# The output projection of a decode step turned over: wo as the stationary operand, its own PSUM columns, and no wait for the row maximum

## Chip, cores, metric

One NeuronCore of a Trainium2 chip. The metric is the device time of one execution in microseconds (us); the median of several is quoted.

## The reference

Two batches, one query token each, 32 heads of 128, a cache of 4096 keys. The gate mixes attention with a small feed-forward.

```python
q = (x @ wq).reshape(B, 1, 32, 128)                 # D = 512
scores = einsum("bhqd,bhkd->bhqk", q, k_cache) * 128**-0.5
o = einsum("bhqk,bhkd->bhqd", softmax(scores), v_cache)
a = o.reshape(B, 1, 4096) @ wo                      # the output projection, 4096 x 512
b = relu(x @ w1) @ w2                               # Dff = 1376
g = sigmoid((x * gate_w).sum(-1, keepdims=True))
out = g * a + (1 - g) * b
```

K and V are 1 MiB per batch and head, 134 MB together; all loads are 146 MB.

## The kernel before

There are 64 items (batch, head). Even items ("G") take their scores on GpSimd (product with a broadcast q) and VectorE (sum), odd items ("P") on TensorE (transposes of K, evictions, matmuls). (An eviction copies a matmul's result out of PSUM; a slot is a buffer that one item's K or V is loaded into.) The engines run one tick per item; item `i` is transposed at tick `i`, its V product comes at tick `i + 4`, and its head is projected at tick `i + 5` if `i` is of the second batch. So all 32 projections fall on ticks 37 to 68. SyncE issues K into 8 slots, ScalarE issues V into 4.

```python
def pe_AO(pe, h):                       # output projection of one head, both batches
    ...                                 # waits for both scaled outputs and for wo
    wait(pe, semGmax, mrow_emitted[0])  # the row maximum must have left psR
    if ao_emitted[0] >= 1:
        wait(pe, semAOacc, ao_emitted[0])
    pe.matmul(psR[32:32 + Bn, 0:Dout], Osb[:, h, :], wo_sb[:, h, :],
              start=True, stop=True).then_inc(semAO, 1)

def pe_MROW(pe, qi):                    # row of partial maxima, into the same psR
    wait(pe, semRmax, qi + 1); wait(pe, semGmax, qi)
    if ao_emitted[0] >= 1:
        wait(pe, semAOacc, ao_emitted[0])
    ...

def dve_AOacc(dve):                     # a_sb[2, 512] += psR
    ...
# TensorE, tick t: T(t) blocks 0,1 | scores(t-1) | T block 2 | MROW(t-2) | MBC(t-3)
#                  | T block 3 | PV(t-4) | AO
# VectorE, tick t: eviction, reductions of item t-1, row max, GMAX(t-2),
#                  OSC(t-4) (reciprocal, scaling), AOacc
# feed-forward, second layer, once at tick 1:
for fc in range(FC):                    # 11 matmuls, 512 moving columns
    pe.matmul(psS[1][0:Bn, 0:Dout], Hsb[0:m, fc, :], w2_sb[0:m, fc, :], ...)

def issue_V(eng, i):                    # on ScalarE's queue, at tick i + 1
    wait(eng, semPV, (i - NVS + 1) * rep)      # slot freed by its V product; NVS = 4
    eng.dma_start(Vs[i % NVS], ...)
def issue_K(eng, i):                    # on SyncE's queue
    knat_slot_free_wait(eng, i)         # slot freed by item i - 8; NKS = 8
    eng.dma_start(Knat[i % NKS], ...)
```

Of the kernel before, what the change touches and what calls it, by code (L numbers as in the profile page):

```python
# [6 lines left out]
ACT = mybir.ActivationFunctionType  # L7
ALU = mybir.AluOpType
AX = mybir.AxisListType
BF16 = mybir.dt.bfloat16  # L10
# [19 lines left out]
def _build(nc, A_x, A_k_cache, A_v_cache, A_wq, A_wo, B_w1, B_w2, gate_w, out,  # L30
# [9 lines left out]
    assert Hq * Dh == HqDh and Hkv * rep == Hq  # L40
    assert Dout <= 512 and D <= 512 and Bn <= 32
    NDC = D // 128
# [4 lines left out]
    NI = Bn * Hkv  # L47
# [7 lines left out]
    NMC = 16  # L55
    MBC0, OT0, DEN0 = 128, 128 + NMC, 128 + 2 * NMC
    inv = 1.0 / math.sqrt(Dh)

# [29 lines left out]
    with es:  # L88
# [28 lines left out]
        x_sb = sb([Bn, D], BF16, "x_sb")  # L117
        gw_sb = sb([Bn, D], BF16, "gw_sb")
        zt = sb([Bn, 4], FP32, "zt")
        bffn = sb([Bn, Dout], FP32, "bffn")  # L120
        a_sb = sb([Bn, Dout], FP32, "a_sb")
        tmp_f = sb([Bn, Dout], FP32, "tmp_f")
        junk = sb([Bn, max(D, Dout)], BF16, "junk")
        outsb = junk[:, 0:Dout]

# [43 lines left out]
        semAOacc = sem("semAOacc")  # L169
        semFin = sem("semFin")  # L170

        block = es.enter_context(nc.Block())
# [20 lines left out]
        def wait(eng, s, v):  # L193
            if v > 0:
                eng.wait_ge(s, v)
# [113 lines left out]
        @block.sync  # L309
        def _(sync):  # L310
            sync.dma_start(x_sb[0:Bn, :], A_x[:, 0, :]).then_inc(semX, 16)
            gw2 = gate_w.rearrange("(o d) -> o d", o=1)
            for b in range(Bn):
                sync.dma_start(gw_sb[b:b + 1, :], gw2[0:1, :]).then_inc(semX, 16)
            for dc in range(0, NDC, 2):
                sync.dma_start(wq_sb[dc][:, :], A_wq[dc * 128:(dc + 1) * 128, :]).then_inc(semWq[dc], 16)
            sync.dma_start(w1_sb[:, :, :], B_w1.rearrange("(c p) f -> p c f", p=128)).then_inc(semW1, 16)
            for t in range(T0, T1):
                issue_tick(sync, "S", t)
            wait(sync, semFin, 2)  # L320
            sync.dma_start(out[:, 0, :], outsb[0:Bn, :]).then_inc(semOut, 16)
            wait(sync, semOut, 16)
# [54 lines left out]

        def pe_AO(pe, h):
            for i in ao_items(h):
                for qi in qis_of_item(i):  # L380
                    wait(pe, semO, qi + 1)
            wait(pe, semWo[h // HO], 16)
            wait(pe, semGmax, mrow_emitted[0])
            if ao_emitted[0] >= 1:
                wait(pe, semAOacc, ao_emitted[0])
            pe.matmul(psR[32:32 + Bn, 0:Dout], Osb[:, h, :], wo_sb[:, h, :],  # L386
                      start=True, stop=True).then_inc(semAO, 1)
            ao_emitted[0] += 1
# [3 lines left out]
        def pe_MROW(pe, qi):  # L392
            wait(pe, semRmax, qi + 1)
            wait(pe, semGmax, qi)
            if ao_emitted[0] >= 1:
                wait(pe, semAOacc, ao_emitted[0])
            if qi == 0:
                wait(pe, semF1b, 2)
            pe.matmul(psR[0:1, 0:128], rmaxb[:, qi:qi + 1], ident_b[:, :],  # L399
                      start=True, stop=True).then_inc(semMrow, 1)  # L400
            mrow_emitted[0] += 1
# [10 lines left out]
        def pe_PV(pe, qi):  # L412
            i = qi // rep
            s = i % NVS
            par = qi % 2
            k = col_k(qi)
            es_ = qi % NES
            wait(pe, semExp, qi + 1)
            wait(pe, semV[s], 16 * (i // NVS + 1))
            for jj in range(J):  # L420
                pe.matmul(psO[par][:, OT0 + k:OT0 + k + 1], Vs[s][:, jj, :],  # L421
                          E[:, es_, jj:jj + 1], start=(jj == 0), stop=(jj == J - 1))
            pe.matmul(psO[par][:, DEN0 + k:DEN0 + k + 1], ones_b[:, :],  # L423
                      rowsum[:, qi:qi + 1], start=True, stop=True).then_inc(semPV, 1)
# [58 lines left out]

        def dve_AOacc(dve):
            k = aoacc_emitted[0]
            wait(dve, semAO, k + 1)
            if k == 0:
                dve.tensor_copy(out=a_sb[0:Bn, :], in_=psR[32:32 + Bn, 0:Dout]).then_inc(semAOacc, 1)
            else:
                wait(dve, semAOacc, k)  # L490
                dve.tensor_tensor(out=a_sb[0:Bn, :], in0=a_sb[0:Bn, :], in1=psR[32:32 + Bn, 0:Dout],  # L491
                                  op=ALU.add).then_inc(semAOacc, 1)
            aoacc_emitted[0] += 1
# [59 lines left out]
        def _(pe):  # L553
            wait(pe, semX, 16 * (1 + Bn))
            wait(pe, semSetup, 3)
            last = None
            for c in range(NDC):
                last = pe.matmul(psR[:, Bn * c:Bn * c + Bn], x_sb[0:Bn, c * 128:(c + 1) * 128],
                                 ident_b[0:Bn, 0:Bn], start=True, stop=True)
            last.then_inc(semXT, 1)  # L560
            wait(pe, semXT, 2)
            for dc in range(NDC):
                wait(pe, semWq[dc], 16)
            for h in range(Hq):
                for dc in range(NDC):
                    last = pe.matmul(psQB[:, Bn * h:Bn * h + Bn],
                                     wq_sb[dc][:, h * 128:(h + 1) * 128],
                                     xT_sb[:, dc, :], start=(dc == 0), stop=(dc == NDC - 1))
            last.then_inc(semQP, 1)

            def pe_FFN(pe):
                wait(pe, semW1, 16)
                wait(pe, semXT, 2)
                ll = None
                for fc in range(FC):
# [8 lines left out]
                if FC > 1:  # L584
                    wait(pe, semW2b, 16)
                for fc in range(FC):
                    m = 128 if fc < FC - 1 else last_m
                    ll = pe.matmul(psS[1][0:Bn, 0:Dout], Hsb[0:m, fc, :], w2_sb[0:m, fc, :],  # L588
                                   start=(fc == 0), stop=(fc == FC - 1))
                ll.then_inc(semF2, 1)  # L590

            for t in range(T0, T1):
# [17 lines left out]
                for h in ao_tick.get(t, []):  # L610
                    pe_AO(pe, h)
                if t == FFN_TICK:
                    pe_FFN(pe)
            for t in sorted(ao_tick):
                if t >= T1:
                    for h in ao_tick[t]:
                        pe_AO(pe, h)

        @block.vector
        def _(dve):  # L620
# [3 lines left out]
                            ).then_inc(semXT, 1)  # L624
            wait(dve, semX, 16 * (1 + Bn))
            dve.tensor_tensor_reduce(out=junk[0:Bn, 0:D], in0=x_sb[0:Bn, :], in1=gw_sb[0:Bn, :],
                                     scale=1.0, scalar=0.0, op0=ALU.mult, op1=ALU.add,
                                     accum_out=zt[0:Bn, 0:1]).then_inc(semG, 1)
            wait(dve, semQP, 1)
# [4 lines left out]
            def dve_FFN(dve):  # L634
# [7 lines left out]
                wait(dve, semF2, 1)  # L642
                dve.tensor_copy(out=bffn[0:Bn, :], in_=psS[1][0:Bn, 0:Dout]).then_inc(semF2b, 1)

            for t in range(T0, T1):
# [14 lines left out]
                for qi in qis_of_item(t - 2):  # L660
                    dve_GMAX(dve, qi)
                for qi in qis_of_item(t - 4):
                    dve_OSC(dve, qi)
                for h in ao_tick.get(t, []):
                    dve_AOacc(dve)
                if t == FFN_TICK:
                    dve_FFN(dve)
            for t in sorted(ao_tick):
                if t >= T1:
                    for h in ao_tick[t]:  # L670
                        dve_AOacc(dve)
            wait(dve, semG, 2)
            dve.tensor_scalar_add(out=zt[0:Bn, 2:3], in0=zt[0:Bn, 1:2], scalar1=1.0).then_inc(semG, 1)
            wait(dve, semG, 3)
            dve.reciprocal(out=zt[0:Bn, 3:4], in_=zt[0:Bn, 2:3]).then_inc(semG, 1)
            wait(dve, semAOacc, Hq)
            wait(dve, semF2b, 1)
            dve.tensor_tensor(out=tmp_f[0:Bn, :], in0=a_sb[0:Bn, :], in1=bffn[0:Bn, :],
                              op=ALU.subtract).then_inc(semFin, 1)
            wait(dve, semFin, 1)  # L680
            wait(dve, semG, 4)
            dve.scalar_tensor_tensor(out=outsb[0:Bn, :], in0=tmp_f[0:Bn, :], scalar=zt[0:Bn, 3:4],
                                     in1=bffn[0:Bn, :], op0=ALU.mult, op1=ALU.add).then_inc(semFin, 1)

        @block.scalar
        def _(act):
# [7 lines left out]
            if FC > 1:  # L694
                act.dma_start(w2_sb[0:last_m, FC - 1, :], B_w2[(FC - 1) * 128:Dff, :]).then_inc(semW2b, 16)
            for t in range(T0, T1):
                issue_tick(act, "A", t)
# [7 lines left out]
                for g in evg[1:]:  # L705
                    ev_copy(act, t, g, True)
            wait(act, semG, 1)
            act.activation(out=zt[0:Bn, 1:2], in_=zt[0:Bn, 0:1], func=ACT.Exp,
                           scale=-1.0).then_inc(semG, 1)

# [29 lines left out]
```

## Time and profile before

| | kernel before |
|---|---|
| median time | 387.5 us (5 runs, 386.5 to 388.5) |
| profiled span | 385.0 us |
| busy: PE, VectorE, ScalarE, GpSimd | 67%, 67%, 29%, 70% |
| HBM read over the span | 378 GB/s |

No engine is near 100%. The prediction below shows the lines: the row of DMA engines, the chain that ended last (read backwards from the end, each piece released by the one above it), the waits, and the groups. One more view shows how full the load engines are where the chain holds no load: the stretch from 225 to 325 us of the kernel before. Its columns are stretch, length, busy time (instructions) of PE, weight loads, VectorE, ScalarE and GpSimd, the granted clock, the share of the DMA engines, GB/s.

```profile
225.00:325.00 100.00, 75.23 (x1274) 60.09 (x1271) 80.37 (x147) 32.49 (x85) 75.29 (x37) 0.62 1.01 415
```

The engines are full there, at 415 GB/s, and still nothing waits for a load (the waits from 225 to 335 us name none).

### The profile page before, as it was taken

Reading aid. Unit: us, or ns where it says so; the run is one execution under the profiler, and the core shown is the slowest. Engines: PE = TensorE matmul, PEld = TensorE weight load, DVE = VectorE, ACT = ScalarE, POOL = GpSimd, SP = SyncE. Lnnn points to the kernel's source line nnn. Section 1 sums busy time; section 2 is a strip of 40 time slices with the busy share of each in tenths; the row PEclk is TensorE's granted clock in tenths of the full one; section 3 lists DMA queues with packets and bytes.
Section 4 is the critical chain, followed back from the end, with each engine's and each line's share of the span. In section 5 each row is a group of like instructions: output and inputs, shape, how many; then the busy total and the mean of one; then the engine's idle time right before and its main releaser. Section 6 shows DMA issues by size and latency. Waiting matters only on the chain.

```text
span 385.0 us, 11076 instructions
## 1 busy us (share of the span) xinstructions
PE 257.2 (67%) x4539; PEld 210.1 (55%) x4539; DVE 258.6 (67%) x491; ACT 111.7 (29%) x290; POOL 269.5 (70%) x137
## 2 busy tenths in 40 slices
PE   0436688486565736777776677788777767887764
PEld 0323577375454626666665665666555555666542
DVE  0024778676735763677776788877778788877775
ACT  0111333333312322333333333332223323332220
POOL 0069998981994698888888757887777778877200
PEclk9999865666556565666555666665556665556665
DMA  8999999999999999999999999999999999966540
GB/s 313 398 411 412 409 418 400 411 415 405 411 413 417 410 417 423 418 419 421 418 421 420 420 420 419 418 421 420 419 418 398 404 413 405 407 254 220 186 145 2
DMA packets 24460, 146.14 MB, mean 380 GB/s; under 512 B 2294, under 2 KB 6748, under 8 KB 7516
## 3 DMA queue, kind: packets, MB, share of 16 engines
q10 hardware_dynamic: 12496, 72.19, 46.9%
q1 hardware_dynamic: 11628, 72.20, 45.7%
q0 software_dynamic: 288, 1.05, 0.7%
q8 instruction: 37, 0.61, 0.6%
q14 instruction: 11, 0.09, 0.1%
HBM read 145.43 MB, written 0.00 MB: 378 GB/s over the span
## 4 chain that ended last, share of the span: by engine, by line
DMA 48%; DVE 26%; PE 21%; issue 4%; ACTq 0%; SPq 0%; DVEq 0%
DMA Vs<-in_A_v_cache_dram 21%; DVE S_sb L448 20%; DMA Knat<-in_A_k_cache_dram 18%; DMA w_sb<-in_B_w_dram 8%; PE psO L421 6%; PE psR L386 4%; PE psT L339 4%; PE psS L361 3%; DVE workA L438 3%; PE psS L588 1%; PE psR L399 1%; DVE rmaxb L463 1%; DVE gmaxb L467 1%; PE psQB L373 1%; PE psO L409 1%
## 5 line engine op out<-in xcount | busy, mean ns | idle before, releaser
L534 POOL TENSOR_TENSOR Knat<-Knat,qb 128x1024 bf16<-128x1024 bf16 x128 | 267.0, 2117 | 87.8 <-ACT qb L500 55.7
L448 DVE TENSOR_REDUCE S_sb<-Knat 128x8 f32<-128x1024 bf16 x128 | 149.4, 1208 | 0.0
L339 PE MATMUL psT<-ident_b,Knat 128*128 128x128 bf16 x1024 | 120.6, 302 | 13.1 <-DMA Knat<-in_A_k_cache_dram 11.8
L339 PEld LDWEIGHTS psT<-ident_b,Knat 128*128 128x128 bf16 x1024 | 98.0, 139 | 27.4 <-issue 14.7
L436 ACT ACTIVATE workA<-psT 128x1024 bf16<-128x1024 bf16 x64 | 65.5, 1023 | 110.3 <-PE psT L339 110.2
L421 PE MATMUL psO<-E,Vs 128*128 128x1 bf16 x2048 | 63.9, 165 | 32.6 <-DMA Vs<-in_A_v_cache_dram 31.3
L421 PEld LDWEIGHTS psO<-E,Vs 128*128 128x128 bf16 x2048 | 60.7, 103 | 35.7 <-issue 26.4
L438 DVE COPY workA<-psT 128x1024 bf16<-128x1024 bf16 x64 | 43.9, 686 | 26.0 <-PE psT L339 26.0
L475 DVE RECIPROCAL recip<-psO 128x1 f32<-128x1 f32 x64 | 10.2, 159 | 54.7 <-PE psO L423 54.7
L386 PE MATMUL psR<-wo_sb,Osb 128*2 128x512 bf16 x32 | 18.3, 572 | 37.9 <-DVE gmaxb L467 37.1
L361 PE MATMUL psS<-Qall,workA 128*128 128x1 bf16 x1024 | 31.9, 165 | 7.1 <-ACT workA L436 5.5
L361 PEld LDWEIGHTS psS<-Qall,workA 128*128 128x128 bf16 x1024 | 30.4, 102 | 10.0 <-issue 8.2
L500 ACT ACTIVATE qb<-psQB 128x128 bf16<-128x128 f32 x32 | 8.9, 277 | 76.8 <-PE psQB L373 74.8
L509 ACT ACTIVATE nbias<-psO 128x1 f32<-128x1 f32 x64 | 11.0, 171 | 65.2 <-PE psO L409 65.2
L491 DVE TENSOR_TENSOR a_sb<-a_sb,psR 2x512 f32<-2x512 f32 x31 | 21.1, 679 | 9.3 <-PE psR L386 7.7
L399 PE MATMUL psR<-ident_b,rmaxb 128*1 128x128 bf16 x64 | 16.6, 259 | 13.9 <-DVE gmaxb L467 11.2
L386 PEld LDWEIGHTS psR<-wo_sb,Osb 128*2 128x2 bf16 x32 | 2.5, 79 | 39.5 <-issue 37.9
L467 DVE TENSOR_REDUCE gmaxb<-psR 1x1 bf16<-1x128 f32 x64 | 17.7, 276 | 1.1 <-PE psR L399 0.8
L399 PEld LDWEIGHTS psR<-ident_b,rmaxb 128*1 128x1 bf16 x64 | 5.1, 79 | 21.4 <-DVE rmaxb L463 13.7
L478 DVE TENSOR_SCALAR Osb<-psO,recip 128x1 bf16<-128x1 f32 x64 | 14.1, 221 | 2.3
L409 PE MATMUL psO<-gmaxb,ones_b 1*128 1x1 bf16 x64 | 11.1, 174 | 1.1
L409 PEld LDWEIGHTS psO<-gmaxb,ones_b 1*128 1x128 bf16 x64 | 6.2, 97 | 9.5 <-issue 3.8
(40 smaller groups left out, 97.3 us busy)
## 6 DMA issues: line engine op xcount, KB each, us to landing
Knat<-in_A_k_cache_dram SPq DMA_DIRECT2D x64, 1024.0 KB, 19.5
Vs<-in_A_v_cache_dram ACTq DMA_DIRECT2D x64, 1024.0 KB, 17.7
workA<-in_A_wq_dram ACTq DMA_DIRECT2D x2, 1024.0 KB, 7.1
workA<-in_A_wq_dram SPq DMA_DIRECT2D x2, 1024.0 KB, 10.5
wo_sb<-in_A_wo_dram SPq DMA_DIRECT2D x3, 512.0 KB, 34.4
wo_sb<-in_A_wo_dram ACTq DMA_DIRECT2D x3, 512.0 KB, 25.9
w_sb<-in_B_w_dram SPq DMA_DIRECT2D x1, 1376.0 KB, 16.2
w_sb<-in_B_w_dram ACTq DMA_DIRECT2D x1, 1280.0 KB, 30.6
```

The lines of the kernel that those rows point to most:

```text
L339: last = pe.transpose(psT[bank][:, c * 128:(c + 1) * 128], Knat[s][:, jj, :], ident_b[:, :])
L361: last = pe.matmul(psS[par][:, col:col + 1], KT[s][:, jj * 128:(jj + 1) * 128], Qall[:, h, b:b + 1], start=True, stop=True)
L386: pe.matmul(psR[32:32 + Bn, 0:Dout], Osb[:, h, :], wo_sb[:, h, :], start=True, stop=True).then_inc(semAO, 1)
L399: pe.matmul(psR[0:1, 0:128], rmaxb[:, qi:qi + 1], ident_b[:, :], start=True, stop=True).then_inc(semMrow, 1)
L409: pe.matmul(psO[par][:, MBC0 + k:MBC0 + k + 1], ones_b[0:1, 0:128], gmaxb[0:1, qi:qi + 1], start=True, stop=True).then_inc(semMbc, 1)
L421: pe.matmul(psO[par][:, OT0 + k:OT0 + k + 1], Vs[s][:, jj, :], E[:, es_, jj:jj + 1], start=(jj == 0), stop=(jj == J - 1))
L436: eng.activation(out=dst, in_=src, func=ACT.Copy).then_inc(semEvA, 1)
L438: eng.tensor_copy(out=dst, in_=src).then_inc(semEvD, 1)
L448: dve.tensor_reduce(out=S_sb[:, ss, q * JQ:(q + 1) * JQ], in_=Knat[s][:, q * JQ:(q + 1) * JQ, :], axis=AX.X, op=ALU.add).then_inc(semRed, 1)
L467: dve.tensor_reduce(out=gmaxb[0:1, qi:qi + 1], in_=psR[0:1, 0:128], axis=AX.X, op=ALU.max).then_inc(semGmax, 1)
L491: dve.tensor_tensor(out=a_sb[0:Bn, :], in0=a_sb[0:Bn, :], in1=psR[32:32 + Bn, 0:Dout], op=ALU.add).then_inc(semAOacc, 1)
L534: pool.tensor_tensor(out=Knat[s][:, q * JQ:(q + 1) * JQ, :], in0=Knat[s][:, q * JQ:(q + 1) * JQ, :], in1=qb_sb[gidx % NQB][:, None, :].bro ...
```

## The change

Intent: take a slow wait out of the second half. The projection's result goes to spare columns of the V product's PSUM tensor, `[128, 8]` instead of `[2, 512]`, with wo as the stationary operand (the one loaded as weights, past which the other's columns move). It is issued ahead of the V product, without the waits for the maximum and the accumulation. Feed-forward, gate and final mix follow the turned-over shape.

```diff
-        def pe_AO(pe, h):
+        def pe_AO(pe, h, par):
             ...
             wait(pe, semWo[h // HO], 16)
-            wait(pe, semGmax, mrow_emitted[0])
-            if ao_emitted[0] >= 1:
-                wait(pe, semAOacc, ao_emitted[0])
-            pe.matmul(psR[32:32 + Bn, 0:Dout], Osb[:, h, :], wo_sb[:, h, :],
-                      start=True, stop=True).then_inc(semAO, 1)
+            for c in range(NOC):
+                ll = pe.matmul(psO[par][:, AOC0 + c * Bn:AOC0 + (c + 1) * Bn],
+                               wo_sb[:, h, c * 128:(c + 1) * 128],
+                               Osb[:, h, :], start=True, stop=True)
+            ll.then_inc(semAO, 1)
 ... pe_MROW
-            if ao_emitted[0] >= 1:
-                wait(pe, semAOacc, ao_emitted[0])
 ... pe_PV
             wait(pe, semExp, qi + 1)
+            for h in ao_tick.get(qi + 4, []):
+                pe_AO(pe, h, par)
             wait(pe, semV[s], 16 * (i // NVS + 1))
 ... dve_AOacc, now ahead of OSC
-            wait(dve, semAO, k + 1)
+            wait(dve, semPV, t - 3)                # (semAO at the last tick)
-                dve.tensor_tensor(out=a_sb[0:Bn, :], ..., in1=psR[32:32 + Bn, 0:Dout], ...)
+                dve.tensor_tensor(out=aT_acc[:, :, :], ..., in1=src, ...)   # 128 x 8
 ... feed-forward, second layer
-                    ll = pe.matmul(psS[1][0:Bn, 0:Dout], Hsb[0:m, fc, :], w2_sb[0:m, fc, :], ...)
+                    ll = pe.matmul(psS[1][:, c * Bn:(c + 1) * Bn],
+                                   w2_sb[0:m, fc, c * 128:(c + 1) * 128], Hsb[0:m, fc, :], ...)
 ... cut: gate computed at the start with matmuls; mix on [128, 8]; four matmuls and a
     copy that turn the result back to [2, 512] before the store
```

More of the change, by code (lines that the diff above doesn't have):

```diff
@@ L40, in _build @@
     assert Hq * Dh == HqDh and Hkv * rep == Hq
-    assert Dout <= 512 and D <= 512 and Bn <= 32
+    assert Dout <= 512 and D <= 512 and Bn <= 32 and Dout % 128 == 0
+    NOC = Dout // 128
     NDC = D // 128
@@ L56, in _build @@
     MBC0, OT0, DEN0 = 128, 128 + NMC, 128 + 2 * NMC
+    AOC0 = 192
+    GWC0, ZC0, GBC0 = 192, 200, 208
     inv = 1.0 / math.sqrt(Dh)
@@ L117, in _build @@
         x_sb = sb([Bn, D], BF16, "x_sb")
-        gw_sb = sb([Bn, D], BF16, "gw_sb")
-        zt = sb([Bn, 4], FP32, "zt")
-        bffn = sb([Bn, Dout], FP32, "bffn")
-        a_sb = sb([Bn, Dout], FP32, "a_sb")
-        tmp_f = sb([Bn, Dout], FP32, "tmp_f")
-        junk = sb([Bn, max(D, Dout)], BF16, "junk")
-        outsb = junk[:, 0:Dout]
+        gw_row = sb([1, D], BF16, "gw_row")
+        gwT_sb = sb([128, NDC], BF16, "gwT_sb")
+        grow = sb([1, 8], FP32, "grow")
+        grow_b = sb([1, Bn], BF16, "grow_b")
+        gbc_sb = sb([128, Bn], FP32, "gbc_sb")
+        aT_acc = sb([128, NOC, Bn], FP32, "aT_acc")
+        bT_sb = sb([128, NOC, Bn], FP32, "bT_sb")
+        tmpT = sb([128, NOC, Bn], FP32, "tmpT")
+        outT = sb([128, NOC, Bn], BF16, "outT")
+        outsb = sb([Bn, Dout], BF16, "outsb")
         psT = [ps([128, 1024], BF16, f"psT{g}") for g in range(2)]
@@ L170, in _build @@
         semFin = sem("semFin")
+        semFinD = sem("semFinD")
         block = es.enter_context(nc.Block())
@@ L312, in _ @@
             gw2 = gate_w.rearrange("(o d) -> o d", o=1)
-            for b in range(Bn):
-                sync.dma_start(gw_sb[b:b + 1, :], gw2[0:1, :]).then_inc(semX, 16)
+            sync.dma_start(gw_row[0:1, :], gw2[0:1, :]).then_inc(semX, 16)
             for dc in range(0, NDC, 2):
@@ L319, in _ @@
                 issue_tick(sync, "S", t)
-            wait(sync, semFin, 2)
+            wait(sync, semFin, 3)
             sync.dma_start(out[:, 0, :], outsb[0:Bn, :]).then_inc(semOut, 16)
@@ L382, in pe_AO @@
             wait(pe, semWo[h // HO], 16)
-            wait(pe, semGmax, mrow_emitted[0])
-            if ao_emitted[0] >= 1:
-                wait(pe, semAOacc, ao_emitted[0])
-            pe.matmul(psR[32:32 + Bn, 0:Dout], Osb[:, h, :], wo_sb[:, h, :],
-                      start=True, stop=True).then_inc(semAO, 1)
+            ll = None
+            for c in range(NOC):
+                ll = pe.matmul(psO[par][:, AOC0 + c * Bn:AOC0 + (c + 1) * Bn], wo_sb[:, h, c * 128:(c + 1) * 128],
+                               Osb[:, h, :], start=True, stop=True)
+            ll.then_inc(semAO, 1)
             ao_emitted[0] += 1
@@ L482, in _build, with dve_AOacc @@
         aoacc_emitted = [0]
-        def dve_AOacc(dve):
+        def dve_AOacc(dve, t):
             k = aoacc_emitted[0]
-            wait(dve, semAO, k + 1)
+            if t - 4 < NI:
+                wait(dve, semPV, t - 3)
+            else:
+                wait(dve, semAO, k + 1)
+            src = psO[t % 2][:, AOC0:AOC0 + NOC * Bn].rearrange("p (c b) -> p c b", b=Bn)
             if k == 0:
-                dve.tensor_copy(out=a_sb[0:Bn, :], in_=psR[32:32 + Bn, 0:Dout]).then_inc(semAOacc, 1)
+                dve.tensor_copy(out=aT_acc[:, :, :], in_=src).then_inc(semAOacc, 1)
             else:
                 wait(dve, semAOacc, k)
-                dve.tensor_tensor(out=a_sb[0:Bn, :], in0=a_sb[0:Bn, :], in1=psR[32:32 + Bn, 0:Dout],
+                dve.tensor_tensor(out=aT_acc[:, :, :], in0=aT_acc[:, :, :], in1=src,
                                   op=ALU.add).then_inc(semAOacc, 1)
@@ L553, in _ @@
         def _(pe):
-            wait(pe, semX, 16 * (1 + Bn))
+            wait(pe, semX, 32)
             wait(pe, semSetup, 3)
@@ L559, in _ @@
                                  ident_b[0:Bn, 0:Bn], start=True, stop=True)
+            for c in range(NDC):
+                last = pe.matmul(psR[:, GWC0 + c:GWC0 + c + 1], gw_row[0:1, c * 128:(c + 1) * 128],
+                                 ident_b[0:1, 0:1], start=True, stop=True)
             last.then_inc(semXT, 1)
+            wait(pe, semXT, 3)
+            for dc in range(NDC):
+                last = pe.matmul(psR[0:1, ZC0:ZC0 + Bn], gwT_sb[:, dc:dc + 1], xT_sb[:, dc, :],
+                                 start=(dc == 0), stop=(dc == NDC - 1))
+            last.then_inc(semG, 1)
             wait(pe, semXT, 2)
@@ L569, in _ @@
             last.then_inc(semQP, 1)
+            wait(pe, semG, 4)
+            pe.matmul(psR[:, GBC0:GBC0 + Bn], ones_b[0:1, 0:128], grow_b[0:1, 0:Bn],
+                      start=True, stop=True).then_inc(semG, 1)
             def pe_FFN(pe):
@@ L573, in pe_FFN @@
                 wait(pe, semXT, 2)
+                wait(pe, semG, 6)
                 ll = None
@@ L585, in pe_FFN @@
                     wait(pe, semW2b, 16)
-                for fc in range(FC):
-                    m = 128 if fc < FC - 1 else last_m
-                    ll = pe.matmul(psS[1][0:Bn, 0:Dout], Hsb[0:m, fc, :], w2_sb[0:m, fc, :],
-                                   start=(fc == 0), stop=(fc == FC - 1))
+                for c in range(NOC):
+                    for fc in range(FC):
+                        m = 128 if fc < FC - 1 else last_m
+                        ll = pe.matmul(psS[1][:, c * Bn:(c + 1) * Bn], w2_sb[0:m, fc, c * 128:(c + 1) * 128],
+                                       Hsb[0:m, fc, :], start=(fc == 0), stop=(fc == FC - 1))
                 ll.then_inc(semF2, 1)
@@ L610, in _ @@
                 for h in ao_tick.get(t, []):
-                    pe_AO(pe, h)
+                    if t - 4 >= NI:
+                        pe_AO(pe, h, t % 2)
                 if t == FFN_TICK:
@@ L616, in _ @@
                     for h in ao_tick[t]:
-                        pe_AO(pe, h)
+                        pe_AO(pe, h, t % 2)
+            wait(pe, semFin, 1)
+            wait(pe, semExp, NQ)
+            for c in range(NOC):
+                ll = pe.matmul(psS[0][0:Bn, c * 128:(c + 1) * 128], outT[:, c, :], ident_b[:, :],
+                               start=True, stop=True)
+            ll.then_inc(semFin, 1)
         @block.vector
@@ L624, in _ @@
                             ).then_inc(semXT, 1)
-            wait(dve, semX, 16 * (1 + Bn))
-            dve.tensor_tensor_reduce(out=junk[0:Bn, 0:D], in0=x_sb[0:Bn, :], in1=gw_sb[0:Bn, :],
-                                     scale=1.0, scalar=0.0, op0=ALU.mult, op1=ALU.add,
-                                     accum_out=zt[0:Bn, 0:1]).then_inc(semG, 1)
+            dve.tensor_copy(out=gwT_sb[:, :], in_=psR[:, GWC0:GWC0 + NDC]).then_inc(semXT, 1)
+            wait(dve, semG, 2)
+            dve.tensor_scalar_add(out=grow[0:1, Bn:2 * Bn], in0=grow[0:1, 0:Bn], scalar1=1.0).then_inc(semG, 1)
+            wait(dve, semG, 3)
+            with nc.allow_low_precision("gate value in bf16 (reference computes the gate in bf16)"):
+                dve.reciprocal(out=grow_b[0:1, 0:Bn], in_=grow[0:1, Bn:2 * Bn]).then_inc(semG, 1)
+            wait(dve, semG, 5)
+            dve.tensor_copy(out=gbc_sb[:, :], in_=psR[:, GBC0:GBC0 + Bn]).then_inc(semG, 1)
             wait(dve, semQP, 1)
@@ L642, in dve_FFN @@
                 wait(dve, semF2, 1)
-                dve.tensor_copy(out=bffn[0:Bn, :], in_=psS[1][0:Bn, 0:Dout]).then_inc(semF2b, 1)
+                dve.tensor_copy(out=bT_sb[:, :, :],
+                                in_=psS[1][:, 0:NOC * Bn].rearrange("p (c b) -> p c b", b=Bn)
+                                ).then_inc(semF2b, 1)
             for t in range(T0, T1):
@@ L661, in _ @@
                     dve_GMAX(dve, qi)
+                for h in ao_tick.get(t, []):
+                    dve_AOacc(dve, t)
                 for qi in qis_of_item(t - 4):
                     dve_OSC(dve, qi)
-                for h in ao_tick.get(t, []):
-                    dve_AOacc(dve)
                 if t == FFN_TICK:
@@ L670, in _ @@
                     for h in ao_tick[t]:
-                        dve_AOacc(dve)
-            wait(dve, semG, 2)
-            dve.tensor_scalar_add(out=zt[0:Bn, 2:3], in0=zt[0:Bn, 1:2], scalar1=1.0).then_inc(semG, 1)
-            wait(dve, semG, 3)
-            dve.reciprocal(out=zt[0:Bn, 3:4], in_=zt[0:Bn, 2:3]).then_inc(semG, 1)
+                        dve_AOacc(dve, t)
             wait(dve, semAOacc, Hq)
             wait(dve, semF2b, 1)
-            dve.tensor_tensor(out=tmp_f[0:Bn, :], in0=a_sb[0:Bn, :], in1=bffn[0:Bn, :],
-                              op=ALU.subtract).then_inc(semFin, 1)
-            wait(dve, semFin, 1)
-            wait(dve, semG, 4)
-            dve.scalar_tensor_tensor(out=outsb[0:Bn, :], in0=tmp_f[0:Bn, :], scalar=zt[0:Bn, 3:4],
-                                     in1=bffn[0:Bn, :], op0=ALU.mult, op1=ALU.add).then_inc(semFin, 1)
+            dve.tensor_tensor(out=tmpT[:, :, :], in0=aT_acc[:, :, :], in1=bT_sb[:, :, :],
+                              op=ALU.subtract).then_inc(semFinD, 1)
+            wait(dve, semFinD, 1)
+            wait(dve, semG, 6)
+            dve.tensor_tensor(out=tmpT[:, :, :], in0=tmpT[:, :, :],
+                              in1=gbc_sb[:, None, :].broadcast_to([128, NOC, Bn]),
+                              op=ALU.mult).then_inc(semFinD, 1)
+            wait(dve, semFinD, 2)
+            dve.tensor_tensor(out=outT[:, :, :], in0=tmpT[:, :, :], in1=bT_sb[:, :, :],
+                              op=ALU.add).then_inc(semFin, 1)
+            wait(dve, semFin, 2)
+            dve.tensor_copy(out=outsb[0:Bn, :], in_=psS[0][0:Bn, 0:Dout]).then_inc(semFin, 1)
         @block.scalar
@@ L695, in _ @@
                 act.dma_start(w2_sb[0:last_m, FC - 1, :], B_w2[(FC - 1) * 128:Dff, :]).then_inc(semW2b, 16)
+            wait(act, semG, 1)
+            act.activation(out=grow[0:1, 0:Bn], in_=psR[0:1, ZC0:ZC0 + Bn], func=ACT.Exp,
+                           scale=-1.0).then_inc(semG, 1)
             for t in range(T0, T1):
@@ L706, in _ @@
                     ev_copy(act, t, g, True)
-            wait(act, semG, 1)
-            act.activation(out=zt[0:Bn, 1:2], in_=zt[0:Bn, 0:1], func=ACT.Exp,
-                           scale=-1.0).then_inc(semG, 1)
     return nc
```

## The prediction

> **What bounds the kernel now.** One core, 64 attention items (two batches of 32 heads). Even items go through GpSimd and VectorE (product on POOL, sum in L448), odd items through TensorE transposes (L339) and their evictions. I call one item of each kind a pair; the program's loop does one item per tick. I read the 40-slice table first, then the chain that ended last, then the waits, then the groups.
>
> ```profile
> DMA  8999999999999999999999999999999999966540
> GB/s 313 398 411 412 409 418 400 411 415 405 411 413 417 410 417 423 418 419 421 418 421 420 420 420 419 418 421 420 419 418 398 404 413 405 407 254 220 186 145 2
> ```
>
> The DMA engines look full until slice 34 (337 us), then fall off for 48 us. Taken alone, this says "DMA-bound, with a tail". The chain says otherwise:
>
> ```profile
> 180.73 18.67 DMA Vs<-in_A_v_cache_dram
> 199.53 1.00 PE psO L421 x32
> 200.59 20.00 DMA Vs<-in_A_v_cache_dram
> 220.72 0.99 PE psO L421 x32
> ...
> 342.82 2.33 DVE S_sb L448 x2
> 345.16 0.60 DVE workA L438
> 345.75 2.26 DVE S_sb L448 x2
> 348.43 0.25 issue
> 348.67 0.38 PE psR L386
> 349.28 0.98 PE psS L361 x32
> 350.57 0.94 PE psO L421 x32
> 351.54 0.52 PE psR L386
> 352.06 0.98 PE psT L339 x8
> 353.23 0.44 issue
> 353.67 2.33 DVE S_sb L448 x2
> ```
>
> Until 221 us the chain is a load of V, its product, the next load into the same of four slots: 19.9 us from one L421 to the next of that slot (179.67 to 199.53 in the same view), so about 5.0 us per item, 10.0 us per pair. That is also what bytes say: a pair loads 4 x 1.049 = 4.19 MB, and 4.19 MB at 419 GB/s is 10.0 us. From 221 us to the end the chain holds no DMA at all: it alternates VectorE and TensorE, and one pair takes 353.67 - 342.82 = 10.85 us. What is new from there is the output projection (L386): a head can be projected only when both batches have it, so all 32 fall into the second half, one per tick, the first at 229 us. In that half the DMA engines are still full because K is fetched up to eight items ahead; that lead is of no use at the end, which is why the GB/s row collapses after 337 us while the compute chain runs on.
>
> ```profile
> PE psR L386 <- DVE gmaxb L467: 26.5, 10, 3.0
> ```
>
> This is from the waits between 225 and 335 us: ten times, once a pair, the projection's matmul holds TensorE for up to 3.0 us, because it shares PSUM tensor psR with the max row that VectorE reduces only after its four big reductions. TensorE is in order, so the scores (L361) behind it wait as well.
>
> ```profile
> L386 PE MATMUL psR<-wo_sb,Osb 128*2 128x512 bf16 x32 | 18.3, 572 | 37.9 <-DVE gmaxb L467 37.1
> L491 DVE TENSOR_TENSOR a_sb<-a_sb,psR 2x512 f32<-2x512 f32 x31 | 21.1, 679 | 9.3 <-PE psR L386 7.7
> L566 PE MATMUL psQB<-xT_sb,workA 128*128 128x2 bf16 x128 | 3.5, 165 | 7.8 <-DMA workA<-in_A_wq_dram 7.8
> L622 DVE CAST xT_sb<-psR 128x8 bf16<-128x8 f32 x1 | 0.2, 165 | 6.5 <-PE psR L558 6.5
> ```
>
> The first two rows are what the change replaces, the last two have the shapes that it puts there.
>
> **What the Trainium skill says.** "TensorE: Matmul & The Clock Gate", section "Wait — 56ns, not 53.3ns?": a matmul's start-to-start time is its moving columns over the array clock, with a floor of some 25 ns. The trace agrees: the 512-column matmuls of the feed-forward part follow each other every 0.43 us, and 128 two-column ones (L566, weights swapped each time) take 3.55 us together, 28 ns each. "Perfetto Trace Analysis", section "Optimizing Scalar/DVE Operations": a VectorE instruction has a fixed overhead, about 125 ns on PSUM, and about twice that as profiled latency. Together with one element per cycle per partition ("VectorE: DVE Perf Modes", section "Mode 1× (REGULAR) — the baseline") a 2x512 add costs by its 512 columns though only two partitions work. The trace: 679 ns for 512 columns, 165 ns for 8; 514 ns for 504 columns, about 1.02 ns each. "DMA: Bandwidth & Descriptors", section "Issuing engines are not separate DMA queues": the K and V queues share the same 16 engines. The trace agrees: 419 GB/s is reached by both together, 46.9% and 45.7% of the engines.
>
> **The change part by part.** (1) The projection is turned over: wo is the stationary operand, four 128x128 blocks with two moving columns. Estimate from L566: 4 x 28 = 0.11 us in the stream in place of 0.38 to 0.58. (2) Its result is 128x8, so the accumulation on VectorE becomes about 0.17 us (L622) in place of 0.68. (3) It leaves psR for spare columns of psO, and is issued just ahead of the V product of the same parity: TensorE no longer waits for the max (the 26.5 us above), and the max row no longer waits for the accumulation. The projection waits for the previous item's scaled output, but the matmul before it (L409) does so already, so that wait isn't new. (4) The feed-forward's second layer: 11 matmuls of 0.43 us become 44 of 28 ns, 4.3 to about 1.2 us, once, at 35 us; there the engines have K queued deep (slices 3 and 4 at 412 and 409 GB/s), so I count zero. (5) The gate is worked out at the start, a few instructions of about 0.2 us, under the first loads: zero. (6) The end has three small adds in place of two long ones, but four matmuls and a 2x512 copy for turning the result back.
>
> Compute time of a pair afterwards. The pair at 213 to 222 us has no projection, and I follow it in the timeline, taking out its V wait: first reduction 213.12, last ends 218.34 (5.22 us); max, reciprocal and scaling to 219.04; broadcast matmul 219.18, V product possible from 219.4, done 220.4; the transposes' first eight and their eviction take 1.66 us to the next reduction (221.60 to 223.26), so 222.06. That is 8.94 us. Add one short accumulation (0.1 to 0.17) and four short matmuls (0.11): about 9.15 us, against 10.85 now: 1.7 us saved per pair, about 0.9 from the waiting and order and 0.8 from shorter work.
>
> But 9.15 is below the DMA's 10.0 us, so the second half becomes DMA-bound as the first is, and only 0.87 us per pair is gained as long as K and V both load. The last K is issued when item 55 has been used, and with some 3.5 MB of K then outstanding at half of 419 GB/s it is gone some 16 us later, about tick 59. After it, V alone needs 2.5 us per item, and compute sets the pace at 9.15.
>
> Sum: ticks 37 to 59, 11 pairs x 0.87 = 9.6 us. Ticks 59 to 63, 2 pairs x 1.7 = 3.4. After the last reduction (370 us now) there are 13.5 us of chain with five projections; shorter accumulations there save some 2.5, the projection that now comes after a scaled output instead of beside it costs some 0.4 on three ticks, and the shapes at the end cancel: 1.5 net. Together 14.5: 387.5 - 14.5 = 373.0 us.
>
> **Rivals.** (a) The gain is hidden: transfers are full to 337 us, so only the tail can gain, about four pairs' worth and the end, 6 to 8 us: 380 us. For it: the DMA row of nines. Against it: the chain from 221 on has no DMA, and what the engines did there was build a lead. (b) A new wait takes the old one's place: the accumulation now waits for the V product, and in DMA-bound stretches that waits for V, so VectorE stalls in front of the reductions and each later K slot is freed later. Against it: the reciprocal (L475) behind it waits for the same V product already. If the two lock together, I'd expect about 10.4 us per pair, half the gain: 380 us. (c) The loads keep up with compute all along: 16 pairs x 1.7 and the end, about 359 us. Against it: 10.0 us per pair throughout the first half, where compute could have done 8.9. The loads put a floor at 90.7 MB by 221 us, then 55.5 MB at 419 GB/s: 354 us and the last items' work, so this can't be had whole, but a K lead that ends earlier than I think would give 2 to 4 us.
>
> **Range and chances.** From (a) and (b) the upper end, 379; from part of (c) 367. I give 0.87 to faster by over 2% (below 379.75), 0.125 to within 2%, 0.005 to slower: no engine gains work.
>
> **What would show it.** Right: the wait of the projection for the max is gone; the accumulation's mean is 0.15 to 0.2 us; V waits appear in the chain after 221 us, at 10.0 us per pair and about 419 GB/s to some 315 us; pairs of 9.0 to 9.3 us after the last K; a steeper, shorter fall of the GB/s row. Wrong: pairs of over 10.3 us with no DMA in the chain (b), pairs at 10.85 until 330 us (a), or a pace below 9.8 us while K still loads (c).

## The result

The changed kernel took 370.89 us (median of 8 runs, 370.3 to 371.9) against 387.09 us (15 runs of the kernel before beside it). The ratio is 0.9578, 95% interval 0.9564 to 0.9593. A ratio here is the mean time of one kernel's fast runs over that of the other's in the same rounds, so it is not quite the ratio of the medians. All runs used here are fast, that is, undisturbed; they lie within 0.7% of the fastest of their kernel.

The profile of the changed kernel, its row of DMA engines and of GB/s in 40 slices of 9.2 us:

```profile
DMA  8999999999999999999999999999999999999860
GB/s 309 398 408 409 415 414 400 414 411 410 405 412 413 416 415 422 414 423 420 420 417 423 421 415 422 417 420 416 422 418 421 417 421 419 419 417 399 340 250 2
```

The row of nines now reaches slice 36, and the falling end is 28 us instead of 48. The chain that ended last (start, length, what), changed kernel:

```profile
219.69 18.59 DMA Vs<-in_A_v_cache_dram
238.33 1.01 PE psO L427 x32
239.41 18.74 DMA Vs<-in_A_v_cache_dram
...
320.43 18.72 DMA Vs<-in_A_v_cache_dram
339.20 1.02 PE psO L427 x32
...
341.76 2.33 DVE S_sb L454 x2
344.10 0.60 DVE workA L444
344.70 2.26 DVE S_sb L454 x2
...
348.14 0.25 PE psO L391 x4
348.39 0.85 PE psO L427 x32
349.27 0.89 PE psT L345 x8
...
350.79 2.33 DVE S_sb L454 x2
```

The chain of V loads, which ended at 221 us before, now goes on to 339 us, four items every 19.9 us (238.33 to 258.19; two later steps take 20.5 and 20.8). Only the last pair runs free of loads, and it takes 350.79 - 341.76 = 9.03 us. The groups of the new operations, changed kernel:

```profile
L391 PE MATMUL psO<-Osb,wo_sb 128*128 128x2 bf16 x128 | 8.1, 167 | 2.7 <-DVE Osb L484 1.4
L501 DVE TENSOR_TENSOR aT_acc<-aT_acc,psO 128x8 f32<-128x8 f32 x31 | 4.8, 154 | 34.3 <-PE psO L429 33.9
```

The projection (L391 here, L386 before) no longer waits for the maximum; the accumulation takes 154 ns instead of 679. Its 33.9 us of waiting for the V product stand ahead of the reciprocal, which waits for the same product and now waits 34.6 us where it waited 54.7. The sum is larger, as the second half now waits for loads.

Where the 16.1 us of span came from, read off VectorE's first eviction in three pairs (timelines; items 37, 61 and 63), before and after:

```profile
222.65 0.69 DVE L438 COPY workA<-psT 128x1024 bf16<-128x1024 bf16 x1 [0.45 <-PE psT L339]
353.06 0.69 DVE L438 COPY workA<-psT 128x1024 bf16<-128x1024 bf16 x1 [0.29 <-PE psT L339]
363.85 0.69 DVE L438 COPY workA<-psT 128x1024 bf16<-128x1024 bf16 x1 [0.29 <-PE psT L339]
```

```profile
220.57 0.69 DVE L444 COPY workA<-psT 128x1024 bf16<-128x1024 bf16 x1 [0.45 <-PE psT L345]
341.16 0.69 DVE L444 COPY workA<-psT 128x1024 bf16<-128x1024 bf16 x1 [0.38 <-PE psT L345]
350.18 0.69 DVE L444 COPY workA<-psT 128x1024 bf16<-128x1024 bf16 x1 [0.38 <-PE psT L345]
```

| stretch | before | after | saved | predicted |
|---|---|---|---|---|
| start to item 37 | 222.65 | 220.57 | 2.1 | 0 |
| item 37 to 61, 12 pairs | 130.41 | 120.59 | 9.8 | 11.3 (11 pairs x 0.87, one x 1.7) |
| item 61 to 63, one pair | 10.79 | 9.02 | 1.8 | 1.7 |
| item 63 to the end of the span | 21.15 | 18.72 | 2.4 | 1.5 |

So the total was right to 2 us, but partly by luck: the start (2.1 us, counted as zero) and the end (0.9 us more than predicted) make up for the pairs, which gave 1.4 us less. The start looked odd, because the load engines were full before and after at the same rate. Most of the experiments went into it and into how much of the gain the loads hide.

### The profile page after: what moved, and what is told of

It reads as the page before. It is cut to its first block, busy times and chain, and to the rows that moved or that the text cites.

```text
span 368.9 us, 11330 instructions
## 1 busy us (share of the span) xinstructions
PE 245.8 (67%) x4681; PEld 211.1 (57%) x4681; DVE 235.9 (64%) x493; ACT 111.7 (30%) x290; POOL 269.6 (73%) x137
## 4 chain that ended last, share of the span: by engine, by line
DMA 81%; DVE 9%; PE 8%; issue 1%; ACTq 0%; SPq 0%; DVEq 0%
DMA Vs<-in_A_v_cache_dram 52%; DMA Knat<-in_A_k_cache_dram 20%; DMA w_sb<-in_B_w_dram 9%; DVE S_sb L454 6%; PE psO L427 4%; PE psT L345 1%; DVE workA L444 1%; PE psO L391 0%; PE psS L611 0%; DVE Osb L484 0%; PE psR L403 0%; DVE gmaxb L473 0%; PE psO L413 0%; DVE aT_acc L501 0%; PE psS L367 0%
## 5 line engine op out<-in xcount | busy, mean ns | idle before, releaser
L427 PEld LDWEIGHTS psO<-E,Vs 128*128 128x128 bf16 x2048 | 59.6, 102 | 42.5 <-issue 16.8
L367 PE MATMUL psS<-Qall,workA 128*128 128x1 bf16 x1024 | 31.1, 164 | 9.8 <-ACT workA L442 8.8
L367 PEld LDWEIGHTS psS<-Qall,workA 128*128 128x128 bf16 x1024 | 29.3, 99 | 13.2 <-issue 9.5
L481 DVE RECIPROCAL recip<-psO 128x1 f32<-128x1 f32 x64 | 10.1, 157 | 34.6 <-PE psO L429 34.6
L501 DVE TENSOR_TENSOR aT_acc<-aT_acc,psO 128x8 f32<-128x8 f32 x31 | 4.8, 154 | 34.3 <-PE psO L429 33.9
L535 ACT ACTIVATE E<-S_sb,nbias 128x32 bf16<-128x32 f32 x32 | 10.3, 321 | 1.2 <-ACT nbias L519 0.2
L429 PE MATMUL psO<-rowsum,ones_b 128*128 128x1 bf16 x64 | 10.5, 164 | 0.0
## 6 DMA issues: line engine op xcount, KB each, us to landing
Vs<-in_A_v_cache_dram ACTq DMA_DIRECT2D x64, 1024.0 KB, 18.7
w_sb<-in_B_w_dram SPq DMA_DIRECT2D x1, 1376.0 KB, 16.7
```

The lines of the kernel that those rows point to most:

```text
L367: last = pe.matmul(psS[par][:, col:col + 1], KT[s][:, jj * 128:(jj + 1) * 128], Qall[:, h, b:b + 1], start=True, stop=True)
L427: pe.matmul(psO[par][:, OT0 + k:OT0 + k + 1], Vs[s][:, jj, :], E[:, es_, jj:jj + 1], start=(jj == 0), stop=(jj == J - 1))
```

## The experiments

**Control.** The changed kernel again, on the chip of the next three.

> Control: the changed kernel unaltered, on the same chip as the next three. Both theories: ratio to the kernel before 0.956 to 0.960, span near 369 us, first projection tick (transposes) reached near 219.7 us.

Measured: 370.9 us, ratio 0.9566 (0.955 to 0.9583), span 368.9, first eviction of item 37 at 220.43 us. As expected.

**The feed-forward made long again.**

```diff
+                for fc in range(7):
+                    pe.matmul(psS[1][0:Bn, 0:Dout], Hsb[:, fc, :], w2_sb[:, fc, :],
+                              start=True, stop=True)     # overwritten by the real ones
                 for c in range(NOC):
```

> The changed kernel with seven idle 512-column matmuls ahead of the feed-forward's second layer, so that it is as long as in the kernel before (about 4.2 us instead of 1.3). Between the two traces the changed kernel reached the first V-bound product 2.2 us earlier (157.5 instead of 159.8 us), before any projection ran. Theory A (the shorter feed-forward started the K refills earlier and the full DMA queue passed that on): 2 to 3 us slower than the control, V product near 159.5 us. Theory B (what the prediction counted: zero, the 2.2 us come from elsewhere or from chance): within 0.7 us of the control.

Measured: 373.24 us, ratio 0.9624 (0.9607 to 0.9642), so 2.3 us above the control; item 37 at 223.53 us, 3.1 us later than in the control (0.9 are won back at the end, where two pairs instead of one run free of loads). The chain shows the idle matmuls ahead of the real ones:

```profile
35.33 3.15 PE psS L609 x7
38.48 1.22 PE psS L614 x44
```

3.15 us at 35 us cost 2.3 us at the end. Theory A: the early gain is the feed-forward, and the prediction's zero for it was wrong. Why it isn't hidden under full load engines is the question of the slot experiments below: the delay itself is gone by item 7 (58.05 us in the kernel before, 57.90 in the changed one), and comes back at item 23 (151.59 and 149.43).

**The new shape alone, in the old bank and place.**

```diff
-            for h in ao_tick.get(qi + 4, []):      # in pe_PV
-                pe_AO(pe, h, par)
+            wait(pe, semGmax, mrow_emitted[0])     # in pe_AO, now called after PV
+            if ao_emitted[0] >= 1:
+                wait(pe, semAOacc, ao_emitted[0])
-                ll = pe.matmul(psO[par][:, AOC0 ...], ...)
+                ll = pe.matmul(psR[:, AOC0 ...], ...)
 ... pe_MROW waits for semAOacc and dve_AOacc for semAO again, behind OSC
```

> The changed kernel with the projection's new shape, but in its old PSUM tensor psR, its old place after the V product and with its old waits (for the max, for the accumulation). Theory A (prediction: of 1.7 us per pair about 0.9 is waiting and order, 0.8 is shorter work, and loads take 10.0 us per pair): pairs of about 9.9 to 10.1 us in the second half, the wait of the projection for the max back at over 1.5 us per pair, time only 2 to 4 us above the control. Theory B (the wait for the max made the 10.85 us): pairs of 10.5 us or more, time 8 to 12 us above the control.

Measured: 373.89 us, ratio 0.9647 (0.963 to 0.9664), 3.0 us above the control. The waits between 225 and 335 us and a pair of the chain:

```profile
PE psR L394 <- DVE gmaxb L476: 27.2, 11, 2.5
```

```profile
303.10 2.33 DVE S_sb L457 x2
...
308.95 0.25 PE psR L394 x4
...
313.31 2.33 DVE S_sb L457 x2
```

A pair takes 10.21 us and again holds no load. So of the 1.87 us between 10.89 and 9.02, the shape gives 0.68 and the rest, order and waits, 1.19 (predicted: 0.8 and 0.9). This run puts back the waits, the PSUM tensor and the order on VectorE together; which of them counts was not tried. Theory A's time holds; its pair time, 9.9 to 10.1, was 0.1 too low. As the loads alone need 9.9, most of the gain is there without the new order (13.7 of 16.7 us, the feed-forward's part included): removing the 27 us wait, the more striking line in the profile, is worth only the last 3 us here. The 2.5 us that TensorE waited per pair weren't 2.5 us of the pair.

**VectorE's work made long again.**

```diff
+            dve.tensor_tensor(out=dmy[0:Bn, :], in0=x_sb[0:Bn, 0:Dout],
+                              in1=x_sb[0:Bn, 0:Dout], op=ALU.add)   # after each accumulation
```

> The changed kernel with an idle 2x512 add on VectorE behind each accumulation, so that VectorE's work per projection is as long as before (about 0.6 us more) while place, waits and TensorE's short form stay. Theory A: pairs of about 10.0 to 10.2 us (9.03 + 2 x 0.55), little above the loads' 10.0, so 2 to 5 us above the control, most of it in the last pairs and the end. Theory B (order alone counts): within 1 us of the control.

Measured: 378.18 us, ratio 0.9752 (0.9736 to 0.9767), 7.3 us above the control, more than either theory said. From item 37 to 63 the pairs average 10.24 us against 9.98 in the control (3.3 us over 13 pairs), the last, free one takes 9.75; from item 63 to the end it is 22.2 us against 18.7, 3.5 us. Two things were wrong in my expectation. The idle add stands ahead of the reciprocal and the scaling, so in the end, where these are the chain, six of them, of 0.6 us each, count in full. And at 9.75 us of work against 9.9 us of loads the add isn't hidden, though work is still the shorter: of the twelve pairs under loads seven take 9.9 us and five 10.2 to 11.2 (in the control three take 10.1 to 10.7). Why stays open. Theory B falls: VectorE's length counts.

**Half of V's bytes, both kernels.** Results are wrong (half a slot keeps an older item's V); the comparison with the reference passed all the same, so its tolerance doesn't see this.

```diff
+            je = J if i < NVS else J // 2
-                Vs[i % NVS][:, :, :], A_v_cache[b, hkv].rearrange(...)
+                Vs[i % NVS][:, 0:je, :], A_v_cache[b, hkv].rearrange(...)[:, 0:je, :]
```

> The kernel before, loading only half of every V item after the first four (wrong results on purpose, the other half of the slot keeps old data; all instructions on the engines stay). Bytes fall from 146 to about 115 MB, so loads allow 7.5 us per pair. Theory A (second half bound by compute at 10.85 us per pair, first half by loads at 10.0): second half unchanged at 10.8 us per pair, first half down to about 8.9, time about 365 us. Theory B (the second half of the kernel before is bound by loads too, its nines in the DMA row): second half falls as well, time below 350 us.

> The changed kernel with the same halved V loads (wrong results on purpose). Theory A (loads at 10.0 us hide part of the gain of 1.7 to 1.8 us per pair): pairs of about 9.0 us in both halves, time about 336 us, some 29 us below the kernel before with the same loads, against 16 us with full loads. Theory B (nothing is hidden, compute alone set the pace): 350 us or more, the difference stays near 16 us.

Measured: 359.63 us (ratio to the full kernel before 0.9288, 0.9274 to 0.9302) and 335.25 us (0.8663, 0.8645 to 0.8682). The stretch from 225 to 325 us in the kernel before with half of V (columns as above):

```profile
225.00:325.00 100.00, 75.22 (x1290) 59.97 (x1287) 79.03 (x149) 31.68 (x85) 77.19 (x37) 0.62 0.68 263
```

The load engines fell from 1.01 to 0.68 and from 415 to 263 GB/s, and the pairs there still take 10.89 us. (The expected 365 us was 5 us too much: item 37 came at 195.78 us.) This shows that the second half of the kernel before was bound by compute although its load engines were full: rival (a) of the prediction, and theory B, fall. In the changed kernel with half of V the 13 pairs from item 37 to 63 average 9.10 us (196.16 to 314.51). The two kernels then differ by 24.4 us in all, against 16.2 with full loads. So the loads do hide a part of the compute gain, as predicted, though I expected 29: with half loads both kernels reach item 37 at the same time (195.78 and 196.16), so the early gain of 2.1 us isn't there.

**K and V slots.** Only `NKS` and `NVS` change (the V issue moves one tick earlier for each V slot more).

```diff
-           NKS=8, NKT=2, NVS=4, ...
+           NKS=6, NKT=2, NVS=6, ...      # or 6 and 4, 8 and 5, 7 and 5
```

> The changed kernel with six K and six V slots in place of eight and four, V issued two ticks earlier. Theory A (loads bind until 340 us, and a K lead of eight items is useless at the end while V comes late): the GB/s row stays at 419 longer, time 2 to 4 us below the changed kernel. Theory B (compute sets the end): within 1 us.

> The kernel before with the same six and six slots. Theory A (its second half is bound by compute): within 1.5 us of the kernel before. Theory B (V slots held it back): 3 us or more faster.

Six and six made the changed kernel 368.61 us (0.9521, 0.9505 to 0.9537), as theory A said: its GB/s row stays at 415 or more to slice 37, where with eight and four it is down to 340. The kernel before took 380.46 us (0.9825, 0.9811 to 0.984). That was a surprise: theory A gave the wrong time and theory B the right one. The second half is bound by compute, as A says, but some 7 us came from the first half. Item 37 came at 215.98 us instead of 222.65, and the pairs after it are 10.89 us as ever. The loads' rate was not higher. Kernel before with 8 and 4 slots, then with 6 and 6, from 60 to 220 us (stretches as above, then waits):

```profile
60.00:150.00 90.00, 54.70 (x1036) 47.36 (x1036) 56.03 (x108) 26.60 (x71) 69.58 (x35) 0.59 1.02 412
150.00:220.00 70.00, 51.66 (x938) 43.78 (x935) 50.54 (x98) 24.24 (x63) 57.73 (x29) 0.60 1.01 419
```

```profile
PE psO L421 <- DMA Vs<-in_A_v_cache_dram: 29.9, 11, 7.0
POOL Knat L534 <- DMA Knat<-in_A_k_cache_dram: 10.8, 2, 9.2
```

```profile
60.00:150.00 90.00, 58.98 (x1085) 51.01 (x1086) 57.63 (x112) 27.74 (x72) 66.43 (x33) 0.59 1.02 411
150.00:220.00 70.00, 55.86 (x1010) 47.57 (x1007) 54.76 (x104) 26.75 (x68) 60.05 (x30) 0.61 1.01 420
```

```profile
POOL Knat L534 <- DMA Knat<-in_A_k_cache_dram: 36.3, 9, 9.2
PE psO L421 <- DMA Vs<-in_A_v_cache_dram: 4.2, 4, 1.6
```

412 and 419 GB/s against 411 and 420: the same bytes, yet TensorE did more (x1036 and x938 matmuls against x1085 and x1010). With eight K slots part of the bytes is K that isn't needed yet, while V is waited for (29.9 us); with six and six V is hardly waited for (4.2 us), and the waiting moved to K (36.3 us). The DMA packets in the traces, added up by queue, bear this out: by item 37 ScalarE's queue (V and some weights) had brought 40.8 and 41.1 MB, SyncE's (K and some weights) 48.8 MB with eight and four slots and 45.8 with six and six. The same work was reached with 3 MB less of K. Two further runs part fewer K slots from more V slots:

> The kernel before with six K slots instead of eight, V slots left at four. Six and six made it 7 us faster by reaching the first projection 6.7 us earlier at the same GB/s. Theory A (eight K slots let K's loads take bandwidth from the V that is waited for): fewer K slots alone give most of that, 4 to 7 us. Theory B (V's four slots hold V back, K's lead does no harm): no gain, within 1.5 us of the kernel before or slower.

> The kernel before with a fifth V slot (V issued one tick earlier) and K left at eight. Theory A (share of the two queues): some gain, 2 to 4 us, since V's outstanding loads rise from four to five against K's. Theory B (the V slots alone): 3 to 7 us. If no gain, the fewer K slots were what mattered in the run with six and six.

Measured: 382.09 us (0.9861, 0.9828 to 0.9894), item 37 at 218.49 us, and 382.51 us (0.9875, 0.9847 to 0.9903), item 37 at 218.32 us. Fewer K slots alone give 5.4 us, one V slot more alone 5.0. Either makes K lead less, and either helps: by item 37 SyncE's queue had brought 46.7 and 47.0 MB, ScalarE's 41.2 and 40.8. Theory A for the first run. The second came out a little above A's 2 to 4 us and alone would fit B, but B can't explain the first.

> The changed kernel with seven K and five V slots, between its own eight and four and the six and six that gained 2.3 us. In six and six the last pair waited 2.2 us for K while the last V lay ready. Theory A (the order of the last loads matters): 366 to 368.5 us, at least as good as six and six. Theory B (nothing left but bytes): 368 to 371 us.

Measured: 368.78 us (0.9516, 0.9488 to 0.9543). It equals six and six; it lies 0.3 us outside theory A's range and inside B's, too close to tell them apart.

**The long feed-forward with six and six slots.** If a late feed-forward costs time because it delays the issue of V while K's queue takes the bandwidth, it must cost little where K leads less.

> The seven idle feed-forward matmuls again (they cost 2.2 us with eight K and four V slots), now in the changed kernel with six and six slots (368.6 us without them). Theory A (a late feed-forward delays the issue of V, and K's deep queue takes the bandwidth meanwhile, so with more V slots and a smaller K lead it costs little): 368.4 to 369.4 us. Theory B (three microseconds more on TensorE early are lost whatever the slots): 370.5 to 372 us.

Measured: 368.78 us (0.9512, 0.9495 to 0.953), against 368.61 us (0.9521) without the idle matmuls: nothing, where the same edit cost 2.3 us with eight and four slots. Theory A; whether the fewer K or the more V slots do it was not tried apart. The bytes by item 37 agree: ScalarE's queue had brought 40.8 to 41.0 MB in each of these runs. With eight and four slots SyncE's had brought 48.8 MB in the kernel before, 47.8 in the changed one and 49.0 in it with the long feed-forward; with six and six slots it is 45.8 with and without the idle matmuls. So the late feed-forward costs time by the K that is loaded ahead of V (1 MB, some 2.4 us at 410 GB/s by estimate), and not by a delay that is handed on. How the delay turns into that lead stays open. The changed kernel is fastest with six and six or with seven and five slots, 368.6 and 368.8 us, 2 us below eight and four.

## Why the prediction was right

- **The bound.** The second half of the kernel before was bound by a chain of VectorE and TensorE, not by its full load engines. Shown: with a third of the load engines' time freed its pairs stayed at 10.89 us.
- **Shape and order.** Predicted 0.8 and 0.9 us per pair; measured 0.68 and 1.19. A free pair was predicted at 9.15 us and took 9.03. Its base was too long: pairs without a projection take 8.73 us when free (half of V, items 25 to 37), not 8.94, so what the projection adds is 0.3 us, not 0.2.
- **The loads take over at 10.0 us.** Shown by the chain of V loads to 339 us, pairs averaging 10.05 us from item 37 to 61, and by half loads, where the gain grows from 16.2 to 24.4 us. They held to tick 61, two ticks longer than I worked out, which takes 0.8 us from this term; with the 10.05 it gave 9.8 + 1.8 = 11.6 us instead of 13.0. (The prediction's 0.87 per pair is 0.85 by its own 10.85 and 10.0.)
- **The end.** Predicted 1.5, measured 2.4 us. From the last reduction to the first of the last four V products it is 1.1 us shorter, the four V products come at the same spacing in both (5.97 and 6.03 us over three ticks: the shorter add and the later projection cancel), and from the last V product to VectorE's last instruction it is 3.9 instead of 5.3 us. The prediction counted the five shorter adds, but not that the projections get shorter too (0.5 to 0.6 us in the chain before, 0.25 after). By its own terms, 2.5 less three times 0.4, it should have said 1.3.
- **The step that failed** is "there the engines have K queued deep [...] so I count zero". It took full load engines to mean that time lost on TensorE is covered. It was 2.1 us. Full engines only say that bytes flow, not that they are the next ones needed: with the late feed-forward K's queue had brought 1 MB more by item 37 and V's the same. Shown by the run that puts 3.15 us back (+2.3 us), by the same edit with six and six slots (+0.2 us, within noise) and by the bytes of each queue. With six and six slots, or half of V, the zero would have been right.
- **Rivals.** (a) and (b) did not happen: with the accumulation's new wait for the V product the pairs stayed at the loads' pace, 10.05 us on average (b: 10.4). Two of them took 10.9 and 10.6 us; why was not looked into. (c) is what half of V's bytes brings about.

The gate's move to the start, and the end's single parts, weren't tried alone. The first doesn't delay the feed-forward, which starts at 34.76 us before and 34.83 after; more the runs don't say, as the long feed-forward puts back 3.1 us at item 37 where 2.1 were gained.

## What to carry to other kernels

A row of nines on the load engines doesn't make a stage load-bound: look whether the chain holds a load there, and test by taking bytes away. A prefetch ring that runs further ahead than needed competes with the load that is waited for, so split slots between streams by which one waits, at no cost in memory. When a change frees compute next to a load bound, work out the loads' pace first and count the gain only down to it; work close to that pace still costs something, as the idle add shows.

## What the Trainium skill lacked or had wrong

- "Perfetto Trace Analysis", section "Identifying the Most-Contended Engine", judges DMA by HBM utilization and then asks which DMA resource binds. In the kernel before that says loads from start to 337 us (415 GB/s from 225 to 325 us), yet with loads cut to 263 GB/s the pairs stayed at 10.89 us. It lacks that prefetch into slots keeps the row full without binding.
- "DMA: Bandwidth & Descriptors", section "Issuing engines are not separate DMA queues", says that the queues interleave; it lacks what follows for two streams of unequal depth. At the same 411 to 420 GB/s, six K slots instead of eight gave 5.4 us, one V slot more 5.0, both (six and six) 7 us.
- "TensorE: Matmul & The Clock Gate", section "Wait — 56ns, not 53.3ns?", agreed: 44 two-column matmuls took 1.31 us (30 ns each, against its floor of some 25).
- "Perfetto Trace Analysis", section "Optimizing Scalar/DVE Operations", agreed in part: the 128x8 add from PSUM took 154 ns, near its overhead of about 125 ns, but that is already the profiled time, which the page puts at about twice the overhead.
